# GpSimd's DMA queue in place of SyncE's for the preparations of chunks 4 to 9 of a recurrent attention kernel

## The chip, the cores and the metric

The kernel runs on one core of a Trainium2 chip. The metric is the device time of one execution in microseconds (us); less is better. Engines are named TensorE (PE in the profile), VectorE (DVE), ScalarE (ACT), GpSimd (POOL) and SyncE (SP). A DMA is begun by an instruction on the queue of one of these engines; SP does nothing but begin DMAs and wait.

## The reference

A linear recurrence over 768 steps for 4 x 8 heads of width 40, followed by two feed-forward parts over all 3072 tokens:

```python
for t in range(S):
    y[:, :, t] = einsum('bhd,bhde->bhe', rt, state)
    Sa = einsum('bhde,bhe->bhd', state, at)
    state = state * wt[:, :, None, :] - einsum('bhd,bhe->bhde', Sa, bt)
    state = state + einsum('bhd,bhe->bhde', vt, kt)
...
x = y.transpose(0, 2, 1, 3).reshape(B * S, H * D)
x = ((x @ w1) * (x @ w2) @ w3) @ w_out            # 320 -> 1024 -> 1024 -> 320
h = maximum(x @ w_in, 0)                          # 320 -> 2048
return h * h @ w_out2                             # 2048 -> 320
```

## The kernel before, in words

The recurrence is cut into 24 chunks of 32 steps. A chunk c needs a **preparation** that does not depend on the state. `prep` (L816) loads the chunk's image of k, b, a and w (`prep_load` L525: `im` at L538 in two parts, or for chunks 1, 2, 3 and 5 one load with w in it at L531; `iw`, the w part, at L548), scans w twice on VectorE (`prep_scan` L550: `suf` L553, `wi` L563, which at its end begins the load of the next chunk's `iw`), multiplies a by `wi` (L575) and k and b by `suf` (four of L581) on GpSimd (VectorE for chunks 0 to 3), and stores both to DRAM (`AW_d`, L582 and L583). `prep_pq` (L585) multiplies them on TensorE (L594); ScalarE copies one part to `Pn` (L598), VectorE transposes the other (`qt`, L599), GpSimd masks it from chunk 4 on (L601), and it is stored as `Q_d` (L602). `prep_kb` (L604) transposes k and b on TensorE (L611), ScalarE copies them to `kn` (L615), and they are stored as `KB_d` (L616). `im`, `iw`, `wi`, `qt` and `kn` have one buffer each from chunk 4 on (chunk 5 alone has another for `im`). `solve` (L621) inverts the triangular systems of four chunks at once, in a chain of small VectorE instructions (L653, L656).

The **state** then goes through each chunk in order: `do_x0` (L732, matmuls L739, copy X0 L741), `do_sa` (L744: L749, copy SA L751), `do_sat` (L753: L756, L758, L761), `do_l` (L763: L769, L774), `do_z` (L778), `do_ys` (L788: matmuls L797, results L805 and L809, store L812). Their inputs come back from DRAM by `load_x` (L703), `load_rv` (L722) and `load_y` (L712), all on SP's queue.

**Beside it** the weights come in and are decoded. `fetch` (L295) loads 64-bit words by SP (L319) into `raw` or `early` buffers; ScalarE (L325, L326) and VectorE (L328, L330) make float32 of them. w3 and w_out are folded into one matrix (L459), w1 and w2 are split in two parts (`split_w` L334, `split_r` L343, with subtractions on GpSimd), and from then on the first feed-forward part is worked in tiles of 256 tokens (`a_tile` L373: `ab` L370, `px` L428) as they leave the recurrence. These pieces stand in a list (`Fill` L73); `stage` (L827) writes one step of the recurrence and then pulls pieces worth so many ns from the list. The second feed-forward part (`ph` L370, `po` L994) follows at the end.

TensorE's order is that of the program, written by hand: `OPENING` (L28) holds the preparations 0 to 4, `BETWEEN` (L32) puts those of 5 to 9 between the steps of chunks 0 to 3, and from chunk 4 on the loop at L874 prepares chunk c + 6. All other engines' orders, SP's and POOL's too, come from a list scheduler with priorities, and an instruction that waits holds all behind it on its engine.

The queue on which a preparation begins its DMAs is a variable, `q_["prep"]` (L523). It is SP's from the start, and the loop sets it to POOL's at L880, where it prepares chunk 10, the first of its own. So all DMAs of L531, L538, L548, L582, L583, L602 and L616 are SP's for chunks 0 to 9 and POOL's after them, but for `iw` of chunk 10, which the scan of chunk 9 begins on SP.

Of the kernel before, what the change touches and what calls it, by code (L numbers as in the profile page):

```python
# [243 lines left out]
def body(tc, img, rv, rd, vn, vp, raw, w1, w2, w3t, wo, win, wo2, ident, maskt, out, dbg=None):  # L244
    nc = tc.nc
    mm = nc.tensor.matmul
    act, dve, pool, sp = nc.scalar, nc.vector, nc.gpsimd, nc.sync

    with (
# [12 lines left out]
        with right, tc.manual_schedule(engines={mybir.EngineType.PE}):  # L262
# [229 lines left out]
            with (  # L492
# [30 lines left out]
                q_ = {"prep": sp}  # L523
# [292 lines left out]
                def prep(p, eng=pool):  # L816
                    with tc.high_priority(offset=SECOND):
                        if p not in pr:
                            prep_load(p)
                        prep_scan(p)  # L820
                        prep_mul(p, eng)

                def solve_all(k, blocks=1):
                    with tc.high_priority(offset=SECOND):
                        return [it() for it in solve(k, blocks)][C // blocks + 3]

                def stage(fn, *a, gap=0):  # L827
                    with tc.high_priority(offset=FIRST):
                        fn(*a)
                    fill.pull(gap)  # L830
# [11 lines left out]

                def run(what):
                    for op, *a in what:
                        if op == "prep":
                            prep(a[0], dve if a[0] in PD else pool)
                        elif op == "pq":
                            stage(prep_pq, a[0], a[0] % 4)
                        elif op == "kb":
                            stage(prep_kb, *a)  # L850
                        elif op == "corner":
                            for b in range(2):
                                if len(a) == 1 or a[1] == b:
                                    stage(corner, a[0], b)
                        elif op == "solve":
                            marks[a[0]] = solve_all(a[0], 1 if a[0] else 2)
                        elif op == "pull":
                            fill.pull(a[0])
                run(OPENING)
                solved = marks[0]  # L860
                YI = at.tile([128, NU, 72], F32, name="YI")
# [12 lines left out]
                for c in range(NCH):  # L874
                    last = c == NCH - 1
                    p = c + 6
                    gaps = (GAP0, GAP1, GAP2, GAP3)[c] if c < 4 else GAPS if c < CUT[0] else GAPM if c < CUT[1] else GAPE
                    more = lambda name: run(BETWEEN.get((c, name), ()))
                    if c > 3 and p < NCH:
                        q_["prep"] = pool  # L880
                        prep(p)
                    more("start")
                    stage(do_x0, c, gap=gaps[0])
                    if not last:
                        stage(load_x, c + 1)
                    more("x0")
                    stage(do_sa, c, gap=gaps[1])
                    more("sa")
                    stage(do_sat, c, gap=gaps[2])
                    more("sat")  # L890
                    stage(do_l, c, gap=gaps[3])
                    if not last:
                        stage(load_rv, c + 1)
                    more("l")
                    if c:
                        stage(do_z, c, gap=gaps[4])
                        more("z")
                    if c > 3 and p < NCH:
                        stage(prep_pq, p, p % 4, gap=gaps[5])
                        stage(prep_kb, p, gap=gaps[6])  # L900
                        if p % 4 == 3:
                            solve_all(p // 4)
                    stage(do_ys, c, last, gap=gaps[7])
                    if not last:
                        stage(load_y, c + 1)
                    more("ys")
                    if c % 2:
                        a_tile(c // 2)
# [225 lines left out]
```

## Time and profile before

| | |
|---|---|
| median of 3 runs | 1076.19 us (1075.29 to 1082.97) |
| profiled execution | 1078.62 us, span 1076.7 us |
| TensorE busy | 917.4 us (85%) |
| VectorE busy | 714.0 us (66%) |
| ScalarE busy | 442.1 us (41%) |
| GpSimd busy | 233.3 us (22%) |

The span is the time from the first to the last instruction of the profiled execution; its own time is 1.9 us longer, and 2.4 us over the median of the runs. The chain that ended last is 52% TensorE, 23% VectorE and 12% DMA. Busy times leave out the issue of DMAs; a wait is named by what came last before it ended.

### The profile page before, as it was taken

Reading aid. Unit: us, or ns where it says so; the run is one execution under the profiler, and the core shown is the slowest. Engines: PE = TensorE matmul, PEld = TensorE weight load, DVE = VectorE, ACT = ScalarE, POOL = GpSimd, SP = SyncE. Lnnn points to the kernel's source line nnn. Section 1 sums busy time; section 2 is a strip of 40 time slices with the busy share of each in tenths; the row PEclk is TensorE's granted clock in tenths of the full one; section 3 lists DMA queues with packets and bytes.
Section 4 is the critical chain, followed back from the end, with each engine's and each line's share of the span. In section 5 each row is a group of like instructions: output and inputs, shape, how many; then the busy total and the mean of one; then the engine's idle time right before and its main releaser. Section 6 shows DMA issues by size and latency. Waiting matters only on the chain.

```text
span 1076.7 us, 29204 instructions
## 1 busy us (share of the span) xinstructions
PE 917.4 (85%) x12240; PEld 823.3 (76%) x12240; DVE 714.0 (66%) x1399; ACT 442.1 (41%) x942; POOL 233.3 (22%) x304
## 2 busy tenths in 40 slices
PE   1327866689989898988999989879999999999997
PEld 1315544588888888887899879868989889898886
DVE  6864879958975996798589344897455554444432
ACT  2424555343434323433343333785433333333332
POOL 0261224433343343434200000562000000000000
PEclk9999988899999899989999999999999999999999
DMA  8976775666666567765744542666122221000001
GB/s 211 312 228 181 215 238 152 163 177 161 168 158 166 147 154 170 173 152 146 182 119 110 129 97 63 159 182 126 30 61 49 63 48 25 2 25 1 18 8 27
DMA packets 208922, 134.44 MB, mean 125 GB/s; under 512 B 143742, under 2 KB 184063, under 8 KB 208369
## 3 DMA queue, kind: packets, MB, share of 16 engines
q1 hardware_dynamic: 201424, 110.61, 40.3%
q0 software_dynamic: 7072, 21.57, 7.2%
q8 instruction: 98, 1.61, 0.7%
q10 hardware_dynamic: 288, 0.33, 0.1%
q14 instruction: 40, 0.32, 0.1%
HBM read 99.27 MB, written 33.19 MB: 123 GB/s over the span
## 4 chain that ended last, share of the span: by engine, by line
PE 52%; DVE 23%; DMA 12%; issue 4%; ACT 4%; SPq 2%; POOL 2%; ACTq 0%; DVEq 0%; POOLq 0%
PE ph L370 15%; PE po L994 15%; PE ab L370 9%; PE px L428 4%; DVE tmp L653 4%; DVE T L656 4%; PE pat L797 2%; DVE wst L328 2%; DVE yst L809 2%; DVE RX L805 2%; DMA im<-img 2%; DMA raw<-w3t 2%; PE pat L769 2%; DMA AW_d<-wi 2%; PE pat L782 1%
## 5 line engine op out<-in xcount | busy, mean ns | idle before, releaser
L994 PE MATMUL po<-wuh,rl 128*128 128x320 f32 x384 | 117.2, 308 | 1.7 <-DVE rl L981 1.7
L994 PE MATMUL po<-wul,rh 128*128 128x320 f32 x384 | 118.3, 308 | 0.0
L994 PE MATMUL po<-wuh,rh 128*128 128x320 f32 x384 | 118.0, 308 | 0.0
L370 PE MATMUL ab<-xh,w1h 128*128 128x256 f32 x192 | 60.0, 313 | 24.6 <-DVE g L402 23.8
L407 ACT CAST gh<-g 128x256 fp32r<-128x256 f32 x96 | 38.9, 405 | 99.2 <-DVE g L402 99.1
L370 PE MATMUL ph<-xh,wih 128*128 128x512 f32 x192 | 76.0, 396 | 2.8 <-issue 2.8
L370 PE MATMUL ph<-xh,wil 128*128 128x512 f32 x192 | 75.7, 394 | 0.0
L370 PE MATMUL ph<-xl,wih 128*128 128x512 f32 x192 | 75.6, 394 | 0.0
L994 PEld LDWEIGHTS po<-wul,rh 128*128 128x128 f32 x384 | 72.0, 188 | 4.3
L994 PEld LDWEIGHTS po<-wuh,rh 128*128 128x128 f32 x384 | 72.0, 188 | 3.8
L994 PEld LDWEIGHTS po<-wuh,rl 128*128 128x128 f32 x384 | 71.7, 188 | 2.4 <-DVE rl L981 2.2
L428 PE MATMUL px<-wph,gh 128*128 128x320 f32 x192 | 65.6, 342 | 2.7 <-ACT gh L407 2.7
L656 DVE TENSOR_TENSOR T<-T,tmp 128x31 f32<-128x31 f32 (+20 forms) x170 | 65.6, 386 | 3.0
L797 PE MATMUL pat<-YI,YR 128*40 128x72 f32 (+1 forms) x1536 | 57.4, 237 | 11.5 <-ACT kn L615 6.7
L653 DVE TENSOR_TENSOR tmp<-PT,T 128x31 f32<-128x31 f32 (+20 forms) x170 | 64.9, 382 | 3.5
L408 DVE TENSOR_TENSOR gl<-g,gh 128x256 fp32r<-128x256 f32 x96 | 45.1, 470 | 33.1 <-ACT gh L407 32.9
L581 POOL TENSOR_TENSOR im<-im,suf 104x256 f32<-104x256 f32 x80 | 65.6, 849 | 0.0
L797 PEld LDWEIGHTS pat<-YI,YR 128*40 128x40 f32 x1536 | 53.1, 125 | 16.1 <-ACT kn L615 7.3
L428 PE MATMUL px<-wph,gl 128*128 128x320 f32 x192 | 61.3, 319 | 0.8 <-DVE gl L408 0.7
L428 PE MATMUL px<-wpl,gh 128*128 128x320 f32 x192 | 60.9, 317 | 0.0
L370 PE MATMUL ph<-xq,wir 128*128 128x512 f32 x192 | 60.3, 394 | 0.0
L401 ACT COPY a_sb<-ab 128x256 f32<-128x256 f32 x96 | 35.6, 371 | 58.6 <-PE ab L370 58.1
(539 smaller groups left out, 2452.6 us busy)
## 6 DMA issues: line engine op xcount, KB each, us to landing
raw<-w3t SPq DMA_DIRECT2D x16, 512.0 KB
YR<-KB_d SPq DMA_DIRECT2D x48, 160.0 KB
im<-img POOLq DMA_DIRECT2D x28, 240.0 KB, 4.6
wt<-AW_d SPq DMA_DIRECT2D x24, 214.5 KB
raw<-wo SPq DMA_DIRECT2D x16, 320.0 KB
RX<-vp SPq DMA_DIRECT2D x24, 208.0 KB
vs<-rv SPq DMA_DIRECT2D x24, 208.0 KB
KB_d<-kn POOLq DMA_DIRECT2D x14, 320.0 KB, 5.6
```

Of the source, the lines that this page charges most:

```text
L328: dve.scalar_tensor_tensor(out=ou, in0=ou, scalar=3, in1=lo, op0=ALU.logical_shift_left, op1=ALU.bitwise_or)
L370: mm(out=ps, lhsT=seq[i][0], rhs=seq[i][1], start=(i == 0), stop=(i == 7))
L401: act.copy(out=a_sb, in_=ps[:, 0])
L407: act.copy(out=t["gh"][:, ff], in_=g)
L408: dve.tensor_tensor(out=t["gl"][:, ff], in0=g, in1=t["gh"][:, ff], op=ALU.subtract)
L428: mm(out=ps, lhsT=a_, rhs=b_, start=(k == 0 and i == 0), stop=(k == 7 and i == 2))
L581: eng.tensor_tensor(out=kb[:, g, :, :, j], in0=kb[:, g, :, :, j], in1=sg, op=ALU.mult)
L653: dve.tensor_tensor(out=tv, in0=Pv[:, :, s, s + 1:n].unsqueeze(3).to_broadcast(sh), in1=Tv[:, :, s, 0:s + 1].unsqueeze(2).to_broadcast(sh) ...
L656: return dve.tensor_tensor(out=o, in0=o, in1=tv, op=ALU.subtract).ins
L769: mm(out=ps[q:q + 64, 0, 32 * i - q // 2:32 * i - q // 2 + 64], lhsT=vs[0:104, i], rhs=RT[0:104, :, i], start=True, stop=True, tile_positi ...
L797: mm(out=ps[64 * y:64 * y + D, b, 72 * z:72 * z + n], lhsT=YR[:, u], rhs=YI[:, u, 0:n], start=True, stop=True, tile_position=(0, 64 * y))
L994: mm(out=po[j][g], lhsT=a_, rhs=b_, start=(ff == 0 and i == 0), stop=(ff == 15 and i == 2))
```

## The change

The queue is chosen for each entry of the two lists by the chunk's number, and the line in the loop goes:

```diff
                 def run(what):
                     for op, *a in what:
+                        q_["prep"] = sp if a[0] < 4 else pool
                         if op == "prep":
                             prep(a[0], dve if a[0] in PD else pool)
                         elif op == "pq":
...
                     if c > 3 and p < NCH:
-                        q_["prep"] = pool
                         prep(p)
                     more("start")
```

The loads of chunks 0 to 3 are begun ahead of `run` (L832 to L837), on SP as before. The last entry of `BETWEEN` that runs, `("pull", 1000)` of chunk 3, leaves POOL's queue in the variable.

## Rows read from the trace of the kernel before

**Rows 1.** Busy time in four stretches: PE, PEld, DVE, ACT, POOL, then clock, DMA share.

```profile
60.00:140.00 80.00, 46.27 (x1241) 35.52 (x1231) 48.37 (x86) 31.18 (x69) 25.31 (x24) 0.94 0.74 205
140.00:220.00 80.00, 57.19 (x903) 44.67 (x903) 71.98 (x136) 42.95 (x91) 32.49 (x35) 0.82 0.68 184
220.00:300.00 80.00, 71.33 (x1318) 65.52 (x1316) 63.19 (x141) 29.49 (x70) 29.13 (x44) 1.00 0.65 162
300.00:600.00 300.00, 274.26 (x5089) 253.62 (x5089) 230.00 (x531) 115.86 (x273) 93.50 (x144) 0.95 0.61 153
```

**Rows 2.** Waits of TensorE, 0 to 230 us: total, times, longest.

```profile
PE pat L756 <- ACT SA L751: 18.0, 3, 8.7
...
PE pat L594 <- POOL im L575: 10.2, 1, 10.2
...
PE pat L797 <- ACT kn L615: 6.3, 1, 6.3
```

**Rows 3.** Waits of SP's queue, 0 to 200 us.

```profile
SPq L548 <- DVE wi L563: 8.6, 4, 3.7
...
SPq L602 <- POOL qt L601: 6.7, 3, 5.6
...
SPq L616 <- ACT kn L615: 6.0, 1, 6.0
```

**Rows 4.** SP's issues in order of time: start, duration, instruction.

```profile
68.40 0.35 SPq L602 DMA_DIRECT2D Q_d<-qt  x1
...
70.94 1.50 SPq L319 DMA_DIRECT2D raw<-w3t  x3
...
77.71 0.40 SPq L319 DMA_DIRECT2D raw<-w3t  x1
```

**Rows 5.** ScalarE in order of time; in brackets the idle time before.

```profile
82.60 0.67 ACT L326 ACTIVATE raw<-raw 128x512 uint32<-128x512 uint32 x1 [2.12 <-DMA raw<-w3t]
...
83.17 0.40 ACT L751 COPY SA<-pat 128x320 f32<-128x320 f32 x1
...
101.67 0.75 ACT L615 COPY kn<-pat 128x320 f32<-128x320 f32 x2 [4.47 <-DMA KB_d<-kn]
```

**Rows 6.** TensorE in order of time.

```profile
74.28 1.29 PE L749 MATMUL pat<-X,tt 32*32 32x40 f32 x64
...
83.63 1.10 PE L756 MATMUL pat<-idt,SA 128*104 128x128 f32 x4 [8.06 <-ACT SA L751]
```

**Rows 7.** DMA issues on POOL in the main loop, in order of time.

```profile
231.85 0.62 POOL L602 DMA_DIRECT2D Q_d<-qt  x1 [0.30 <-POOL qt L601]
232.46 1.02 POOL L538 DMA_DIRECT2D im<-img  x2
233.47 0.56 POOL L616 DMA_DIRECT2D KB_d<-kn  x1
```

**Rows 8.** VectorE in order of time.

```profile
64.31 2.37 DVE L330 SCALAR_TENSOR_TENSOR wst<-raw,wst 128x512 uint32<-128x512 uint32 x3
...
68.34 1.24 DVE L563 TENSOR_TENSOR_SCAN wi<-im,inv 104x528 f32<-104x528 f32 x1
```

**Rows 9.** GpSimd in order of time.

```profile
57.39 8.75 POOL L581 TENSOR_TENSOR im<-im,suf 104x256 f32<-104x256 f32 x4
66.10 2.27 POOL L601 TENSOR_TENSOR qt<-qt,msk 128x256 f32<-128x256 f32 x1
68.34 3.65 POOL L581 TENSOR_TENSOR im<-im,suf 104x256 f32<-104x256 f32 x4
71.94 1.17 POOL L575 TENSOR_TENSOR im<-im,wi 104x512 f32<-104x512 f32 x1
```

**Rows 10.** The chain that ended last: start, duration, what.

```profile
97.39 4.17 DMA KB_d<-kn
```

**Rows 11.** DMA issues on POOL by line: KB each, median us to landing.

```profile
im<-img POOLq DMA_DIRECT2D x28, 240.0 KB, 4.6
...
KB_d<-kn POOLq DMA_DIRECT2D x14, 320.0 KB, 5.6
```

## The prediction

> **What bounds the kernel now.** I read the busy time by stage first, because the change touches the first 200 us and little else. From 300 to 600 us TensorE is busy 274.26 of 300 us [rows 1], and its program order is fixed by hand, so the end moves only when the early stages move. From 60 to 140 us TensorE is busy 46.27 of 80 us, from 140 to 220 us 57.19 of 80, from 220 to 300 us 71.33 of 80 [rows 1]. What can be won is thus at most 33.7 + 22.8 us of idle TensorE between 60 and 220 us. In the second of these stages VectorE is busy 71.98 of 80 us: there it is the next limit, and there are only 8 us of slack in it.
>
> Second, who TensorE waited for, up to 230 us: 18.0 us for the copy of SA (8.7 the longest), 10.2 us for GpSimd's `im` in the preparation of chunk 5, 6.3 us for the copy of `kn` [rows 2]. Third, what held SP's queue, since the change takes work out of it. Between 0 and 200 us it stood 8.6 us for the scan `wi`, 6.7 us for GpSimd's `qt`, 6.0 us for the copy of `kn` [rows 3]: 21.3 us, all waits of stores and loads of preparations of chunks 4 to 9, and all of them in front of weight loads that were free to go.
>
> The clearest place is 62 to 84 us. SP stands 5.6 us, until 68.40, for the `Q_d` store of chunk 4, which needs GpSimd's `qt` [rows 3, 4]; the three loads of w3t go behind it at 70.94, and the fourth at 77.71, when VectorE has freed the first buffer [rows 4]. ScalarE decodes these loads in order; it waits 2.12 us for the fourth and only at 83.17 comes to the copy of SA behind it [rows 5]. TensorE had finished SA's matmuls at 74.28 + 1.29 = 75.6 us and waited 8.06 us for that copy [rows 6].
>
> **The change part by part.** From the code, the DMAs that go from SP to POOL are, for chunks 4, 6, 7, 8 and 9, two of `iw`, two of `im`, two of `AW_d`, one `Q_d` and one `KB_d`; for chunk 5 one load and four stores; and two `iw` of chunk 10, which are fetched in the scan of chunk 9. That is 40 + 5 + 2 = 47. Nothing is added or removed, and no byte moves that did not move before. `corner`, `solve` and `pull` also pass the new line, but begin no transfer of this queue; from chunk 4 of the main loop on the queue is POOL's as before.
>
> On SP an issue costs some 0.35 us (`Q_d` at 68.40 [rows 4]), so 47 x 0.35 = 16 us of SP's time go, and the 21.3 us of waits with them. On POOL an issue costs 0.51 to 0.62 us (1.02 for two of `im`, 0.56 for `KB_d`, 0.62 for `Q_d` [rows 7]), so POOL gets 47 x 0.55 = 26 us. It is busy 25.31 of 80 us and 32.49 of 80 in the two stages [rows 1]; most of the 26 us lie in idle time, and cost something where GpSimd itself is waited for.
>
> *The stall at 62.8.* Without the `Q_d` wait SP goes on at 62.8 with the loads of chunk 1's x0 (some 2.1 us, as between the end of `Q_d` at 68.75 and 70.94) and could issue w3t at 64.9. The buffers bind now: VectorE's last pass over three staged blocks runs 64.31 to 66.7 [rows 8], so the third load goes at 66.7 in place of 71.97. That is 5.3 us earlier. The fourth hangs on the first by the same decode, so ScalarE gets to SA 5.3 us earlier, at 77.9, still behind the matmuls' end at 75.6. I take -5.3 us. Bounds: -7.6 (the whole of 83.17 - 75.6) and 0 (if ScalarE's order puts another late load ahead).
>
> *Preparation of chunk 5.* TensorE waits for `im` of L575, 71.94 + 1.17 = 73.1 us. GpSimd works without a gap from 57.39: four L581 that take 8.75 us, `qt` 2.27, four more L581 (chunk 6) 3.65, then L575 [rows 9]. It could not run before VectorE's `wi` of 68.34 + 1.24 = 69.6 [rows 8]. The moved issues among these (`Q_d` and `KB_d` of chunk 4, two `im` of chunk 6) cost 4 x 0.55 = 2.2 us if all come before L575; if L575 is put ahead of chunk 6's L581, it gains 71.94 - 69.6 = 2.3. I take 0, bounds -2.3 and +2.2. What hides a loss here: nothing, as TensorE waits on it directly.
>
> *Stores of `KB_d`.* There is one `kn` buffer: ScalarE's next `kn` waits for the store of the last. At 97.39 the store landed after 4.17 us [rows 10], and ScalarE waited 4.47 us for it with X0's copy queued behind [rows 5]. On POOL this store comes behind `Q_d` and two `im` issues (231.85 to 233.47, 1.6 us later than `Q_d` [rows 7]), and its median landing is 5.6 us [rows 11], 1.4 more. At worst this is +3.0 us on TensorE's wait for X0, at best 0 when ScalarE's order changes. I take +2.
>
> *The rest of SP's waits* for `wi`, `qt` and `kn` is 21.3 - 5.6 = 15.7 us [rows 3, 4]: behind them lie loads whose buffers wait for VectorE anyhow, in the stage where it is 90% full [rows 1]. Bounds 0 and -15.7; the nearest row is VectorE's slack of 8 us, of which I take a quarter, -2.
>
> *From chunk 10 on* the queue is unchanged: 0.
>
> Sum: -5.3 + 0 + 2 - 2 = -5.3 us. The profiled execution took 1078.6 us (span 1076.7), 2.4 more than the median of the three runs, 1076.2. So 1073.3 against it, and 1070.9 as a median: 1071, 0.5% less.
>
> A rule that speaks against the change: during the run of 8.75 us GpSimd's four L581 took 2.4 times the 3.65 us of the next four [rows 9], beside VectorE's decode [rows 8]. The DMA issues of rows 7, in a stage where VectorE is 79% busy [rows 1], show no such stretch. The Trainium skill, "SBUF — State Buffer", section "SBUF: two separate sides", warns that GpSimd cannot write the descriptors of its DMAs while VectorE holds the port pair that they share, and gives some 3.1 us in place of 0.62 for one. If that held here, POOL would get an estimated 47 x 3.1 = 146 us and the sum would turn positive; the trace of the later chunks does not bear it out, and the third rival prices the same mechanism from rows.
>
> **The rivals.**
>
> *A larger gain.* All early stalls behind SP shrink, not the one. TensorE's longest waits beside the 8.06 us are 8.7 us for SA and 6.3 us for `kn` [rows 2], both where ScalarE's decode of weights was late. With half to all of these 15.0 us, say 11.7: 1078.6 - 5.3 - 11.7 = 1061.6, as a median 1059. For it: 21.3 us of waits leave SP [rows 3]. Against it: VectorE has 8 us of slack from 140 to 220 us [rows 1].
>
> *No change.* What is won before 140 us is waited for again at VectorE, whose work up to 220 us is the same; then 1076. For it: 71.98 of 80 us [rows 1]. Against: VectorE has 31.6 us idle from 60 to 140 us (48.37 busy of 80), into which work could move.
>
> *Slower: POOL's queue becomes the bound.* POOL takes its instructions in order, so a load waits for its buffer and the multiplication behind it for the landing. In the place from 66 to 73 us: `qt` ends at 68.37, `Q_d` 0.6, two `im` of chunk 6 1.0, landing 4.6 [rows 11], four L581 3.65, L575 ends at 68.4 + 0.6 + 1.0 + 4.6 + 3.65 + 1.17 = 79.4, against 73.1: +6.3 us at TensorE. The `KB_d` store adds up to 3.0 us in each of chunks 5 to 8, half of it 6.0; and issues stretched 2.4 times beside a full VectorE would put 47 x 0.55 x 1.4 = 36 us more on POOL, of which 5% on the path, 2. Together +14 us: 1092.6, as a median 1090. It decides as soon as L575 of chunk 5 ends more than 5.3 us later than now, after 78.4. For it: GpSimd is waited for already (10.2 us). Against: it is idle for more than half of both stages [rows 1], and only chunk 5 has TensorE waiting on it.
>
> That the change does not do what it says I exclude: with `a[0] < 4` every preparation of chunks 4 to 9 gets POOL's queue.
>
> **How the numbers follow.** Forecast 0.36, larger gain 0.28, no change 0.14, slower 0.22. A change of under 1% (10.8 us) can hardly be told from none here: 1065.4 and 1087.0 are the limits. Of the forecast's 0.36, 0.08 lie under 1065.4 (-7.6 - 2.3 + 0 - 2 = -11.9); of the slower case 0.03 stay under 1087. Faster 0.28 + 0.08 = 0.36; slower 0.19; within 1% 0.28 + 0.14 + 0.03 = 0.45. The range goes to 1054 (a little beyond the larger gain) and to 1090 (the slower case), with 0.1 outside at each end. The forecast's own range is 1064 to 1076.
>
> **What would show it.** Right: SP has no `Q_d` or `iw` in 60 to 170 us, w3t is issued near 66 us, ScalarE copies SA near 78 us and TensorE's wait for it is about 3 us in place of 8.06; `ys` of chunk 0 starts near 84 us. Wrong: L575 of chunk 5 ends after 76 us; POOL waits long for landings of `im` or for `kn`; VectorE is over 95% busy from 140 to 220 us and TensorE's 57 us there do not grow; or the gain before 140 us is gone at 300 us. The prediction falls if the time is under 1060 or over 1087.

## The result, and the profile after

| | before | after |
|---|---|---|
| median | 1075.74 us (1074.71 to 1082.97) | 1090.66 us (1086.0 to 1099.62) |
| ratio to before, 95% interval | | 1.0142 [1.0098, 1.0186] |
| profiled execution | 1078.62 us, span 1076.7 us | 1088.97 us, span 1087.1 us |
| GpSimd busy | 233.3 us | 254.2 us |
| bytes by POOL's DMA queue | 21.57 MB | 31.26 MB |
| `ys` of chunks 0, 1, 4 and 23 starts | 89.6, 120.4, 233.3, 671.6 | 88.5, 127.3, 241.0, 681.3 |
| last transpose of `solve(1)` starts | 214.35 | 224.24 |

The medians are of four runs each. The change costs 1.4%. The row of `ys` starts tells where. It wins 1.1 us at chunk 0, has lost 6.9 at chunk 1, 7.7 at chunk 4 and 9.7 at chunk 23; the span is 10.4 longer. So most of the loss arises between `ys` of chunk 0 and that of chunk 1, 38.9 us apart in place of 30.8, and is then carried along. Part of the 10.4 us is not a wait: the same 12240 matmuls in the same order kept TensorE busy for 921.4 us in place of 917.4, at a mean granted clock of 0.949 of full speed in place of 0.958.

Busy times of the kernel after, in the stretches of [rows 1]:

```profile
60.00:140.00 80.00, 43.39 (x1068) 34.10 (x1069) 51.05 (x79) 29.66 (x66) 36.98 (x47) 0.87 0.67 181
140.00:220.00 80.00, 55.05 (x893) 40.83 (x891) 72.30 (x136) 39.48 (x83) 36.35 (x44) 0.88 0.68 187
220.00:300.00 80.00, 71.38 (x1325) 66.21 (x1326) 60.20 (x136) 32.56 (x77) 29.30 (x44) 0.93 0.63 162
```

TensorE did 2.9 us less in the first stretch and 2.1 less in the second. GpSimd's busy time (fifth column) rose by 11.7 in the first; for this engine, unlike SP, it holds the DMA instructions too (the page counts 351 instructions in place of 304, the 47 that were moved). VectorE is as full in the second as it was. TensorE's waits, 0 to 230 us, against [rows 2]:

```profile
PE pat L749 <- ACT raw L326: 9.6, 1, 9.6
PE pat L749 <- ACT X L741: 8.7, 1, 8.7
PE pat L594 <- POOL im L575: 8.5, 1, 8.5
PE pat L756 <- ACT SA L751: 7.2, 2, 4.3
...
PE pat L797 <- DVE YI L774: 4.3, 1, 4.3
```

The wait for SA fell from 18.0 to 7.2 us, the way that was forecast. From 60 us on three others came up: X0 of chunk 1 (8.7), `YI` of chunk 0 (4.3), and 9.6 at chunk 4's `do_sa`. That last row names ScalarE, whose L326 had long been done; what ended then was `solve(1)`, below.

**Chunk 0: the gain, and where it went.** SP after, against [rows 4]:

```profile
66.74 8.05 SPq L319 DMA_DIRECT2D raw<-w3t  x4
```

The loads of w3t go from 66.74 on, 4.2 us earlier than before, as forecast. ScalarE after, in order of time:

```profile
74.75 0.67 ACT L326 ACTIVATE raw<-raw 128x512 uint32<-128x512 uint32 x1
75.58 0.42 ACT L751 COPY SA<-pat 128x320 f32<-128x320 f32 x1 [0.17 <-PE pat L749]
...
80.36 0.66 ACT L326 ACTIVATE raw<-raw 128x512 uint32<-128x512 uint32 x1 [2.47 <-DMA raw<-w3t]
```

SA is copied at 75.58 in place of 83.17 [rows 5]. But the decode of the fourth load of w3t, behind which SA stood before, now stands behind SA, at 80.36. It is only 82.60 - 80.36 = 2.2 us earlier. So the transfers' share of the 7.6 us is what lies between the fourth decodes or the third ones, 2 to 5 us, and ScalarE's order, which the scheduler wrote anew, gave the rest. TensorE after, against [rows 6]:

```profile
73.11 1.18 PE L594 MATMUL pat<-im 40*32 40x64 f32 x64 [8.50 <-POOL im L575]
...
78.20 1.07 PE L756 MATMUL pat<-idt,SA 128*104 128x128 f32 x4 [2.69 <-DVE qt L599]
...
88.48 3.73 PE L797 MATMUL pat<-YI,YR 128*40 128x72 f32 x60 [4.31 <-DVE YI L774]
```

L756 is 5.4 us earlier, `ys` of chunk 0 only 1.1: it waits 4.31 us for `YI`. The chain that ended last shows why:

```profile
68.52 0.72 POOL qt L601
...
69.73 7.28 DMA im<-img
...
80.72 0.70 POOL qt L601
...
81.70 0.60 POOL Q_d L602
...
82.81 2.25 DMA iw<-img
...
85.19 1.27 DVE suf L553
```

This is the queue of POOL at work. A load of `im` lands 7.28 us after its issue; L581 and `qt` follow; the store `Q_d` follows `qt`; and only behind them does POOL begin the load of `iw` of chunk 7, at 82.29, 2.0 us after the `wi` that it needs was done (80.24). VectorE, in its fixed order, waits for it with `YI` behind. Before, SP began that load as soon as `wi` was done, at 81.87. So the work in front of it had come forward by 5 us, and this load had not.

**Chunk 1: 6.9 us lost.** ScalarE after, then SP's weight loads after and before:

```profile
105.69 0.66 ACT L325 ACTIVATE wst<-early 128x512 f32<-128x512 f32 x1 [9.75 <-DMA early<-w]
...
106.80 0.42 ACT L741 ACTIVATE X<-pat 128x320 f32<-128x320 f32 x1
```

```profile
96.94 1.26 SPq L319 DMA_DIRECT2D early<-w  x2
```

```profile
98.27 0.37 SPq L319 DMA_DIRECT2D early<-w  x1
...
106.49 0.35 SPq L319 DMA_DIRECT2D early<-w  x1
```

The first block of w1 is begun 1.3 us earlier than before and decoded later, at 105.69 against 103.92. SP, with less else to do, now begins the second block with the first and not at 106.49, beside POOL's `im`; the DMA engines' share from 96 to 106 us is 1.01, before 0.94. And ScalarE's new order puts this decode ahead of X0, which it used to follow, and the decode of the second block ahead of SA. X0 comes at 106.80 in place of 102.31, SA at 110.11 in place of 105.05. When the same kernel was run again (e11), the first block was decoded at 103.18, no later than before, and X0 came at 104.28; but the second block then held SA to 111.62. What both executions share is the order. Then VectorE after, and GpSimd after:

```profile
109.75 0.68 DVE L330 SCALAR_TENSOR_TENSOR wst<-early,wst 128x512 uint32<-128x512 uint32 x1
110.35 5.76 DVE L330 SCALAR_TENSOR_TENSOR wst<-raw,wst 128x512 uint32<-128x512 uint32 x1
```

```profile
109.99 0.55 POOL L616 DMA_DIRECT2D KB_d<-kn  x1 [10.63 <-ACT kn L615]
110.56 1.19 POOL L575 TENSOR_TENSOR im<-im,wi 104x512 f32<-104x512 f32 x1
111.70 2.62 POOL L581 TENSOR_TENSOR im<-im,suf 104x256 f32<-104x256 f32 x4
114.28 1.28 POOL L341 TENSOR_TENSOR w1l<-wst,w1h 128x512 fp32r<-128x512 f32 x1
```

An instruction of 0.68 us takes 5.76, for as long as GpSimd works without a gap (110.56 to 115.56). It frees the buffer of the next load of w3t, which SP begins at 116.19. ScalarE waits for this load with the copy of `YR` behind it, and TensorE waits for `YR`; ScalarE and TensorE after:

```profile
122.27 0.66 ACT L326 ACTIVATE raw<-raw 128x512 uint32<-128x512 uint32 x1 [6.92 <-DMA raw<-w3t]
```

```profile
127.35 0.46 PE L797 MATMUL pat<-YI,YR 128*40 128x72 f32 x2 [3.44 <-ACT YR L785]
```

Before, `YR` was copied at 117.15, after at 126.61. Of the 6.9 us, 4.5 are there when TensorE goes on behind X0 (L749 at 107.27 in place of 102.81), and 2.5 come after it.

SP's queue shows where its waits went. Before and after, 0 to 200 us:

```profile
SPq L319 <- DVE wst L330: 17.9, 7, 4.1
```

```profile
SPq L319 <- DVE wst L330: 39.5, 12, 5.9
```

The waits of [rows 3] left it, 21.3 us; its waits for VectorE to free a buffer of a weight load grew by 21.6. The loads behind were not free to go.

**Chunk 4: paid at `solve(1)`.** VectorE before and after, first and last transposes of `solve(1)`:

```profile
128.88 2.10 DVE L646 STREAM_TRANSPOSE PT<-Pn 128x256 f32<-128x256 f32 x4
...
214.35 0.60 DVE L659 STREAM_TRANSPOSE tt<-T 128x256 f32<-128x256 f32 x1
```

```profile
136.86 2.17 DVE L646 STREAM_TRANSPOSE PT<-Pn 128x256 f32<-128x256 f32 x4
...
224.24 0.62 DVE L659 STREAM_TRANSPOSE tt<-T 128x256 f32<-128x256 f32 x1
```

`solve(1)` starts 8.0 us later and takes 1.9 longer (87.4 against 85.5). TensorE, which used to come to chunk 4's `do_sa` 1.6 us before its end, now waits 9.6, before and after:

```profile
215.10 1.29 PE L749 MATMUL pat<-X,tt 32*32 32x40 f32 x64 [1.58 <-DVE tt L659]
```

```profile
225.01 1.29 PE L749 MATMUL pat<-X,tt 32*32 32x40 f32 x64 [9.62 <-ACT raw L326]
```

Theory C, from here on: the end of `solve(1)` on a full VectorE sets chunk 4, and with it the span.

### The profile page after: what moved, and what is told of

It is laid out like the page before. It is cut to its first block, busy times and chain, and to the rows that moved or that the text cites. A ratio compares the mean times of both kernels' runs of the same rounds, so it can differ in the third digit from the quotient of the medians.

```text
span 1087.1 us, 29216 instructions
## 1 busy us (share of the span) xinstructions
PE 921.4 (85%) x12240; PEld 827.4 (76%) x12240; DVE 717.2 (66%) x1399; ACT 442.3 (41%) x942; POOL 254.2 (23%) x351
## 3 DMA queue, kind: packets, MB, share of 16 engines
q0 software_dynamic: 10144, 31.26, 10.1%
## 4 chain that ended last, share of the span: by engine, by line
PE 54%; DVE 22%; DMA 12%; issue 4%; ACT 3%; POOL 2%; SPq 1%; ACTq 0%; DVEq 0%; POOLq 0%
PE ph L370 17%; PE po L994 16%; PE ab L370 9%; DVE tmp L653 4%; PE px L428 4%; DVE T L656 4%; PE pat L797 3%; DMA im<-img 2%; DVE yst L809 2%; DVE RX L805 2%; PE pat L769 2%; DMA early<-wo 2%; DMA X_d<-yst 2%; DVE wst L328 2%; DMA early<-w 2%
## 5 line engine op out<-in xcount | busy, mean ns | idle before, releaser
L370 PE MATMUL ph<-xl,wih 128*128 128x512 f32 x192 | 76.7, 399 | 0.0
L653 DVE TENSOR_TENSOR tmp<-PT,T 128x31 f32<-128x31 f32 (+20 forms) x170 | 67.7, 398 | 3.4
L581 POOL TENSOR_TENSOR im<-im,suf 104x256 f32<-104x256 f32 x80 | 64.6, 837 | 5.9 <-DMA im<-img 3.0
L402 DVE TENSOR_TENSOR g<-a_sb,ab 128x256 f32<-128x256 f32 x96 | 39.9, 415 | 36.3 <-ACT a_sb L401 35.5
```

What stands on the lines that cost most here:

```text
L370: mm(out=ps, lhsT=seq[i][0], rhs=seq[i][1], start=(i == 0), stop=(i == 7))
L402: dve.tensor_tensor(out=g, in0=a_sb, in1=ps[:, 1], op=ALU.mult)
L581: eng.tensor_tensor(out=kb[:, g, :, :, j], in0=kb[:, g, :, :, j], in1=sg, op=ALU.mult)
L653: dve.tensor_tensor(out=tv, in0=Pv[:, :, s, s + 1:n].unsqueeze(3).to_broadcast(sh), in1=Tv[:, :, s, 0:s + 1].unsqueeze(2).to_broadcast(sh) ...
```

## The experiments

Each kernel was timed beside the kernel before on the same chip. In the expectations, A and A2 put the loss on the orders that the scheduler writes and on single waits in them, B on POOL's queue holding transfers back, C is the one above; D, E and F are told where they come up.

| kernel | ratio to before, 95% interval | span | last transpose of `solve(1)` | `ys` of chunks 1, 4 |
|---|---|---|---|---|
| before | | 1076.7 | 214.35 | 120.4, 233.3 |
| after | 1.0142 [1.0098, 1.0186] | 1087.1 | 224.24 | 127.3, 241.0 |
| after, again (e11) | 1.0109 [1.0066, 1.0151] | 1085.2 | 226.47 | 128.7, 243.7 |
| loads alone (e1) | 0.9957 [0.9927, 0.9987] | 1064.7 | 200.36 | 119.2, 227.3 |
| stores alone (e2) | 1.0005 [0.9968, 1.0043] | 1074.9 | 206.17 | 118.5, 233.3 |
| chunks 4, 5 (e3) | 1.0048 [1.002, 1.0075] | 1078.4 | 219.00 | 122.7, 239.8 |
| chunks 6 to 9 (e4) | 1.0035 [1.0008, 1.0062] | 1080.2 | 219.35 | 123.8, 238.9 |
| after, X0 first (e5) | 1.0107 [1.0049, 1.0165] | 1082.7 | 224.73 | 127.5, 243.6 |
| after, scan behind `YI` (e6) | 1.0103 [1.0069, 1.0136] | 1084.9 | 226.28 | 127.5, 244.1 |
| after, both (e7) | 1.0073 [1.0033, 1.0112] | 1081.9 | 219.10 | 122.5, 237.7 |
| loads alone, scan behind `YI` (e8) | 0.9974 [0.9944, 1.0004] | 1066.8 | 203.01 | 121.0, 230.8 |
| after, less decode on VectorE (e9) | 1.0075 [1.0046, 1.0103] | 1078.0 | 207.83 | 126.2, 234.4 |
| before, late end of `solve(1)` (e10) | 1.0076 [1.0051, 1.0101] | 1085.8 | 227.93 | 122.3, 245.8 |
| one store (e12) | 1.0012 [0.9985, 1.004] | 1074.4 | 216.65 | 122.2, 233.6 |
| after, one `KB_d` on SP (e13) | 1.007 [1.0036, 1.0104] | 1080.3 | 224.17 | 128.2, 242.9 |
| one store and two loads (e14) | 0.9991 [0.9964, 1.0018] | 1073.7 | 214.18 | 121.6, 234.1 |
| after, all `KB_d` on SP (e15) | 1.0042 [1.0009, 1.0074] | 1080.5 | 221.41 | 124.7, 239.6 |
| loads of `im` alone (e16) | 0.9955 [0.9922, 0.9987] | 1072.3 | 212.73 | 122.1, 232.2 |
| before, SA first (e17) | 1.0016 [0.999, 1.0043] | 1073.2 | 216.14 | 123.3, 234.3 |
| loads alone, SA first (e18) | 0.9931 [0.9907, 0.9954] | 1072.9 | 203.76 | 120.2, 234.3 |

The span and the starts are those of one execution. For e18 this one was the slowest of eleven, so its median, 1068.35 us, says more; for e1 it was the fastest of ten, for e10 the slowest of seven. Single executions scatter: in the five whose orders up to there are those of before, but for one swap on ScalarE in e17 (before, e10, e12, e14, e17), `ys` of chunk 1 starts between 120.4 and 123.3, and the last transpose, in e10 the first of twelve, between 214.2 and 218.8.

**Loads or stores, early or late chunks.** e1 gives the loads of `im` and `iw` alone to POOL, e2 the stores alone, e3 chunks 4 and 5, e4 chunks 6 to 9.

```diff
-                q_ = {"prep": sp}
+                q_ = {"prep": sp, "store": sp}
...
-                    q_["prep"].dma_start(out=Q_d[c], in_=qf.rearrange("p h t -> p (h t)"))
+                    q_["store"].dma_start(out=Q_d[c], in_=qf.rearrange("p h t -> p (h t)"))
```

> Only the loads (im, iw) of chunks 4 to 9 are begun by POOL, the stores by SP. Theory A (the loss is the order that the scheduler wrote on ScalarE: X0's copy of chunk 1 behind the decode of a late w1 load, in the changed kernel): in this kernel's ScalarE order X0 of chunk 1 stands ahead of that decode, so TensorE's wait for it is under 4 us in place of 8.7 and the time is 1072 to 1080. Theory B (POOL's in-order queue: loads wait there for buffers and behind landings): the loads are what waits, so most of the 14.9 us loss stays, 1086 or more.

> Only the stores (AW_d, Q_d, KB_d) of chunks 4 to 9 are begun by POOL, the loads by SP. Theory A: X0 of chunk 1 stands ahead of the w1 decode in ScalarE's order too, 1070 to 1080. Theory B: stores cost POOL 24 issues of 0.55 us, but no landing is waited for there; a third of the loss at most, 1076 to 1082. Parts that add up (e1 plus e2 losses equal the whole, 15 us) speak for B, parts that don't for A.

```diff
-                        q_["prep"] = sp if a[0] < 4 else pool
+                        q_["prep"] = pool if op != "pull" and a[0] in (4, 5) else sp
```

> Only chunks 4 and 5 go over POOL. Theory A: ScalarE's order at X0 of chunk 1 is that of the changed kernel (the decode of the first w1 block ahead of it), so the wait of 8 to 9 us at TensorE stays and the time is 1082 to 1095. Theory B: 13 of 47 transfers are moved, iw of chunk 7 is issued by SP again, so a third of the loss, 1077 to 1082.

> Only chunks 6 to 9 (and iw of chunk 10) go over POOL. Theory A: X0 of chunk 1 stands ahead of the decode, wait under 4 us, 1070 to 1080. Theory B: 32 of 47 transfers are moved and the waits of iw of chunk 7 behind im of chunk 6 are there, two thirds of the loss, 1084 to 1090.

The loads alone win 0.4%, the stores alone nothing that can be measured, the two together lose 1.1 to 1.4%. These parts don't add up, as costs of a queue would. Chunks 4 and 5 and chunks 6 to 9, which each move loads and stores together, each lose about a third; those two do add up within their intervals. In each of the four the list scheduler also wrote other orders for ScalarE and VectorE (in the kernel after, from 57 and from 27 us on; behind 230 us no instruction of theirs stands elsewhere). Of the orders that the expectations name, all four came: TensorE waits 3.5 to 3.9 us for X0 of chunk 1 in e1, e2 and e4, where it stands ahead of the first w1 decode, and 6.0 in e3, where it stands behind.

**Single waits.** e5 puts the decode of the first w1 block behind X0 of chunk 1 on ScalarE, e6 the scan `suf` of chunk 7 behind `YI` of chunk 0 on VectorE, e7 both; e8 makes the second edit in e1. In e6 and e8 the swap is all that differs in the orders; in e5 and e7 ScalarE's and VectorE's differ behind it too, up to 230 us.

```diff
+                with tc.issue_after(x0a[1]) if (tag, count["split"], 1 in x0a) == ("split", 1, True) else nullcontext():
                     act.activation(out=o, in_=hi.bitcast(F32), func=AF.Copy, scale=2.0 ** -112)
...
+                    with tc.issue_after(x0a["l", 0]) if c == 7 else nullcontext():
                         dve.tensor_tensor_scan(
```

> The changed kernel with one order on ScalarE: the decode of the first w1 block is written behind X0's copy of chunk 1. Theory A2 (the loss is the wait of 8.7 us for X0 of chunk 1, and the late ys of chunk 1 then lets solve of chunks 4 to 7 start and end 8 to 10 us later on a full VectorE): the wait is under 4 us, ys of chunk 1 begins before 123 us in place of 127.3, TensorE's wait for that solve at sa of chunk 4 is under 4 us in place of 9.6, and the time is 1076 to 1083. Theory B (POOL's queue itself): the wait moves elsewhere, 1087 or more.

> The changed kernel with one swap on VectorE: the scan of chunk 7, which waits for iw's landing from POOL's queue, stands behind the masked copy YI of chunk 0; all other engines' orders are the same. ys of chunk 0 begins 3 to 4 us earlier (near 85 us). Theory A2: X0 of chunk 1 then still waits for the w1 load, which SP begins behind loads that wait for that ys, so the 3 to 4 us are kept and the time is 1085 to 1088. Theory B: the same 3 to 4 us, since this one wait does come from POOL's queue. If the 3 us are lost at the next wait, 1090.

> Both orders of the two runs before. Theory A2: 1072 to 1080, level with the kernel before or under it. Theory B: 1084 or more.

> Loads alone over POOL (the kernel that took 1071.6) with the scan of chunk 7 behind YI of chunk 0. There TensorE waited 1.1 us for YI; 1069 to 1072 if that is all.

ScalarE in e5:

```profile
99.46 0.44 ACT L741 ACTIVATE X<-pat 128x320 f32<-128x320 f32 x1 [1.45 <-PE pat L739]
108.58 0.66 ACT L325 ACTIVATE wst<-early 128x512 f32<-128x512 f32 x1 [8.69 <-DMA early<-w]
```

X0 is free 7.3 us earlier, and the same load now holds SA behind it: TensorE waits 10.8 us there, and `ys` of chunk 1 stays at 127.5. In e6 `ys` of chunk 0 starts at 86.5, 2 us earlier, which is gone at chunk 1 too. Both together bring chunk 1 to 122.5 and the ratio to 1.0073, about half the loss, with an interval that still overlaps that of e11. Neither wait alone is the cause; ScalarE stands still on this load wherever it comes, and only the copies ahead of it escape. In e1 the second edit wins nothing.

Over all twenty kernels this order goes with the loss at chunk 1. Where SA of chunk 1 stands behind one w1 decode on ScalarE (eleven kernels), `ys` of chunk 1 starts 30.8 to 32.9 us after that of chunk 0; where it stands behind two (the other nine, e5 and e7 among them), 35.0 to 41.0. Two w1 blocks begun together are not enough for it: e1, e2, e4, e8, e16 and e18 begin them so and are of the eleven. But the nine are also those that move loads and stores of chunks 4 and 5, so that order and transfers are not told apart by this.

**Is it `solve(1)`?** e10 puts off nothing but its end: the orders of all engines are those of before up to there. e9 takes VectorE work out of the kernel after: it leaves out VectorE's part of the decode of five weight blocks.

```diff
-                        dve.transpose(out=tt.rearrange("p u t -> p t u")[:, 8 * j:8 * j + 8],
-                                      in_=square(T)[:, 8 * j:8 * j + 8])
+                        for _ in range(12 if (k, j) == (1, 3) else 1): dve.transpose(
+                            out=tt.rearrange("p u t -> p t u")[:, 8 * j:8 * j + 8], in_=square(T)[:, 8 * j:8 * j + 8])
```

> The kernel before, with the last transpose of solve(1) (L659) done twelve times in place of once; every engine's order up to there is that of before, so that nothing but the end of solve(1) is put off, by 4 to 7 us. Theory C: the whole of it is found again at the end, a span near 1082 (+5 us). Theory B, or any theory in which the middle of the kernel is held by transfers with room to spare: nothing of it is found again, a span within 2 us of 1076.7.

VectorE in e10, the first and the last of the twelve, and TensorE in e10:

```profile
218.78 0.61 DVE L659 STREAM_TRANSPOSE tt<-T 128x256 f32<-128x256 f32 x1
...
223.42 5.12 DVE L659 STREAM_TRANSPOSE tt<-T 128x256 f32<-128x256 f32 x8
```

```profile
228.68 1.29 PE L749 MATMUL pat<-X,tt 32*32 32x40 f32 x64 [10.73 <-DVE tt L659]
```

The end came 13.6 us later (228.54 against 214.95), more than the 4 to 7 meant. But the first of the twelve begins at 218.78 already, 4.4 us later than the one of before with the orders of before: that much is scatter of this execution, and TensorE comes as much later itself. The other eleven put the end off by 9.15 us, and TensorE's wait rose by these 9.15 us (10.73 against 1.58); the median rose by 0.76%, 8.2 us. What `solve(1)` alone ends late is paid, nearly whole. Behind the edit ScalarE's and VectorE's orders are other ones too; what these did is not separated.

```diff
-                    dve.scalar_tensor_tensor(out=ou, in0=ou, scalar=3, in1=lo, op0=ALU.logical_shift_left,
+                    if not (early and tag == "split" and count["split"] > 5): dve.scalar_tensor_tensor(out=ou, in0=ou, scalar=3, in1=lo, op0=ALU.logical_shift_left,
...
-                    dve.scalar_tensor_tensor(out=ou, in0=hi, scalar=0x80000000, in1=ou, op0=ALU.bitwise_and,
+                    if not (early and tag == "split" and count["split"] > 5): dve.scalar_tensor_tensor(out=ou, in0=hi, scalar=0x80000000, in1=ou, op0=ALU.bitwise_and,
```

> The kernel after, with the VectorE part of the decode (L328 and L330, ten instructions of 0.68 us) left out for the last five blocks of w1 and w2; what is computed with those blocks is then not the reference's. Theory C (the span is set by the end of solve(1) on a full VectorE, and lies 862 us behind its last transpose, as in the ten kernels so far): the last transpose of L659 comes about 7 us earlier than the 224.2 of after, near 217, and the span is about 5 to 7 us shorter, near 1081. Theory B (POOL's queue holds the transfers back throughout the middle): VectorE's work is not the limit, and the span stays within 3 us of 1087.

The last transpose came 16.4 us earlier, not 7; the orders changed too, from 170 us on. The span fell by 9.1, the ratio to 1.0075, with an interval that overlaps that of e11. TensorE waits no more for `solve(1)`, but still 8.6 us for an X0, 8.0 for `vs` and 7.2 for SA, all copies by ScalarE. So C holds up to the point where `solve(1)` is done in time; what would have to change beyond it was not tried. Over the twenty profiles of the table the span rises by 0.65 us for each us by which the last transpose starts later (correlation 0.89; with the ratios in place of the spans 0.60 us and 0.80). C is the main path and not the only one: in e13 `solve(1)` ends as late as after, and the span is 6.8 us shorter (4.9 against e11).

> The kernel after once more, beside the others on the same chip: a ratio between 1.010 and 1.018, with the last transpose of solve(1) near 224.

As expected; the loss is there again, with an interval that overlaps the first.

**Transfers alone, with the orders of before.** In e12 and e14 the orders of ScalarE, VectorE and TensorE are exactly those of before.

```diff
-                    q_["prep"].dma_start(out=Q_d[c], in_=qf.rearrange("p h t -> p (h t)"))
+                    (pool if c == 4 else q_["prep"]).dma_start(out=Q_d[c], in_=qf.rearrange("p h t -> p (h t)"))
```

> The kernel before, with one transfer alone moved to POOL: the store of Q_d of chunk 4, the one on which SP stood still at 62.8; the orders of ScalarE, VectorE and TensorE are those of before. The forecast's first term: w3t near 66, the copy of SA near 78, ys(0) near 85, and 3 to 5 us less at the end. Theory C: the same start, but the gain is kept only as far as solve(1) on VectorE ends earlier: a last transpose at 212 to 214 and 0 to 2 us less at the end.

SP in e12:

```profile
62.26 2.17 SPq L538 DMA_DIRECT2D im<-img  x1
...
65.42 3.36 SPq L705 DMA_DIRECT2D XL<-AW_d  x2
...
70.24 1.50 SPq L319 DMA_DIRECT2D raw<-w3t  x3
```

The store on which SP stood 5.6 us is gone, and w3t is begun 0.70 us earlier, not 5.3. Two DMA instructions of SP that took 0.32 us and 0.68 us (for two) before now take 2.17 and 3.36. e14 moves the two loads of `im` of chunk 6 as well:

```diff
-                        q_["prep"].dma_start(out=t[r], in_=img[c, r, 0:n])
+                        (pool if c in (6,) else q_["prep"]).dma_start(out=t[r], in_=img[c, r, 0:n])
```

> The kernel before with the store of Q_d of chunk 4 and the two loads of im of chunk 6 begun by POOL, nothing else; the orders of ScalarE, VectorE and TensorE are those of before. The forecast's first term alone, with the second thing on which SP stood still in the run with one store taken away too: w3t near 65, the copy of SA at 77 to 79, ys(0) at 84 to 86. If the 5 us are kept, the span is 1071 to 1073; theory C lets through only what solve(1) ends earlier, which with the order of before on VectorE is 0 to 3 us: a span of 1073 to 1077.

SP in e14:

```profile
57.89 7.24 SPq L727 DMA_DIRECT2D RT<-rv  x2
...
69.52 1.50 SPq L319 DMA_DIRECT2D raw<-w3t  x3
```

The wait went to the instruction before: two loads that took 0.66 us take 7.24, and w3t is begun at 69.52, SA copied at 82.57. In both, the time is that of before. This is the second cover of the first term: with the wait for `Q_d` gone, SP stands longer in other DMA instructions. What holds it there is not shown; that it is its own open transfers is a guess. Long ones occur in every kernel: before, a load of `YI` (L714) takes 2.8 us of SP in the median and up to 5.6. And e12 and e14 move one and three transfers where the change moves 47; no run moves all 47 with the orders of before.

**POOL's wait for `KB_d`.** e13 gives back the one store for which POOL stood 10.63 us, with ScalarE's order unchanged and VectorE's changed in part (117 to 165 us); e15 gives back all `KB_d` of chunks 4 to 9, with both orders changed from 107 us on.

```diff
-                    q_["prep"].dma_start(out=KB_d[c], in_=kn.rearrange("p g z y e -> p (g z y e)"))
+                    (sp if c in (6,) else q_["prep"]).dma_start(out=KB_d[c], in_=kn.rearrange("p g z y e -> p (g z y e)"))
```

> The kernel after with one transfer alone given back to SP: the store of KB_d of chunk 6, for which POOL stood still 10.6 us (to 109.99) with L575, L581 and L341 behind it. The orders of ScalarE and TensorE are those of after, VectorE's differs in 27 lines. Theory D (POOL's in-order wait makes ys(1) late): POOL runs L575 and L581 some 5 to 10 us earlier, no L330 beside them takes over 3 us, ys(1) comes at 123 to 125 in place of 127.5, and the last transpose of solve(1) and the span are 3 to 4 us earlier. Theory E (ScalarE's order: it waits for early<-w to 105.7 whatever POOL does): ys(1) stays at 127 and the span within 2 us of 1087.

> The kernel after with all stores of KB_d of chunks 4 to 9 given back to SP; loads and the stores of AW_d and Q_d stay with POOL. Theory D: POOL's waits for kn are the price of the change, so the time comes near that of the kernel with the loads alone on POOL: a ratio of 0.995 to 1.003. Theory E (each such set writes another order, and the order decides): a ratio anywhere from 1.003 to 1.014.

GpSimd in e13:

```profile
108.40 1.16 POOL L575 TENSOR_TENSOR im<-im,wi 104x512 f32<-104x512 f32 x1 [7.74 <-DMA im<-img]
```

The wait for `kn` gone, the landing of `im` holds the same instruction to 108.40 in place of 110.56. The stretched L330 is shorter (2.42 us at 113.33), but ScalarE waits 10.27 us for the w1 block as before, and `ys` of chunk 1 stays at 128.2. Theory D falls for this wait; E holds at chunk 1. Still the ratio is lower, 1.007, though its interval overlaps both of the kernel after; if that is a gain, it comes in some later part that no row here names. With all of `KB_d` back the ratio is 1.0042: the stores of `KB_d` on POOL, with the orders that come with them, are worth some 0.7% to 1.0%, the largest piece found, and the rest of the change is still no gain. This price hangs on the moved loads: in e2, where the loads stay with SP, all stores on POOL cost nothing that can be measured.

**What the faster set owes.** e16 gives POOL the loads of `im` alone, by the line of e14's second edit with chunks 4 to 9; that line is L538, so the one load of chunk 5 (L531) stays with SP.

> The kernel before with the loads of im of chunks 4 to 9 alone begun by POOL (iw and all stores stay with SP). If the gain of the kernel with both kinds of load on POOL comes from im, which holds 480 KB to 839 KB for each chunk and stays long in flight: a ratio of 0.993 to 0.998 and a last transpose of solve(1) at 200 to 206. If it comes from iw, or from the order written for that set: 0.998 to 1.005.

The same 0.4% as with `iw` too, though the last transpose started only 1.6 us earlier than before, at 212.73 and not at 200 to 206, which is within the scatter. So moving the loads of `im` is enough for that gain, and it does not come by way of `solve(1)` alone. Its orders differ from before as well; whether transfers or order give the 0.4% stays open.

**SA first.** e17 and e18 were to put the copy of SA of chunk 0 ahead of the fourth decode, in before and in e1.

```diff
+                with tc.issue_after(x0a["sa"]) if "sa" in x0a and "done" not in x0a and x0a.setdefault("done", 1) else nullcontext():
                     act.activation(out=o, in_=hi.bitcast(F32), func=AF.Copy, scale=2.0 ** -112)
```

> The kernel before with one thing changed: ScalarE's copy of SA of chunk 0 (L751) stands ahead of the fourth decode of w3t (L326) and not behind it, as it does in the kernel after; no transfer moves, and all other engines' orders are the same. Theory F (of the 7.6 us by which SA came earlier in the kernel after, the order gave what lies between the third and the fourth decode): SA near 80.1 in place of 83.2, ys(0) near 86.6 in place of 89.6. At the end: 3 us less if kept (a ratio near 0.997), nothing if solve(1) on VectorE still decides (0.999 to 1.001).

> The kernel with the loads alone on POOL, with the same swap on ScalarE: SA near 77.6 in place of 80.9, ys(0) near 84.5. If kept to the end, a ratio of 0.992 to 0.995; if solve(1) decides, that of the kernel without the swap, 0.994 to 0.998.

ScalarE in e17:

```profile
83.53 0.66 ACT L326 ACTIVATE raw<-raw 128x512 uint32<-128x512 uint32 x1 [3.80 <-DMA raw<-w3t]
84.09 0.41 ACT L751 COPY SA<-pat 128x320 f32<-128x320 f32 x1
84.40 0.68 ACT L326 ACTIVATE raw<-raw 128x512 uint32<-128x512 uint32 x1
```

The edit caught the wrong block. It acts on the first fetch written after SA, which is that of the third load: its decode stands behind SA at 84.40 and waits for nothing, while the last load, begun at 77.51, still holds SA, to 83.53. So F was not tested. What speaks for it are the rows of the kernels run: SA is copied between 75.5 and 76.7 us in all nine whose order has it ahead of the last load's decode, and between 80.8 and 84.1 in the other eleven; e1, which moves the loads and keeps the decode ahead of SA, copies SA at 80.87, 2.3 us earlier than before. The nine are again those that move loads and stores of chunks 4 and 5. e18 is the fastest kernel here, 0.7% under before, its interval overlapping that of e1.

## Why the prediction was wrong

It said 1071 us; the change gives 1090.66, just above its range and at the time of its slower rival.

*The stall at 62.8 (-5.3).* Right in size at TensorE (-5.4 at L756), but by luck: the cause was another, and so was what it is worth. e12 and e14 show that without the blamed store, and without the next thing in the way, w3t goes 0.7 and 1.4 us earlier: the longer DMA instructions on SP are a second cover under the first. Of the 7.6 us by which SA came earlier, the rows give 2 to 5 to the transfers and the rest to ScalarE's new order, which the forecast had kept. **The step that failed is here**: the 5.3 us at L756 were booked at the end without asking what `ys` of chunk 0 waits for next. That was `YI`, behind a load of `iw` that POOL began late, and 1.1 us were left (0.1 in e11).

*Preparation of chunk 5 (0).* Right in the number: L594 starts at 73.11 against 73.17. It is the sum of two shifts: L575 was put ahead of chunk 6's L581, as the lower bound has it, and VectorE's `wi` was done 2.2 us later (71.79 against 69.58).

*Stores of `KB_d` (+2).* Mis-sized. The forecast looked at the store's landing, which holds ScalarE; the wait that came was POOL's own for `kn`, with loads and multiplications behind it (10.63 us at 109.99). Between e15 and the kernel after lie 0.7 to 1.0%, 7 to 11 us, the changed orders included.

*The rest of SP's waits (-2).* No such gain came. "In front of weight loads that were free to go" was a wrong reading: 21.3 us of waits left SP's queue, and its waits for buffers that VectorE frees grew by 21.6. At chunk 1, where the sum had nothing but this term and the one before, the change lost 8.1 us between two `ys`. ScalarE's new order had two w1 decodes ahead of SA where one had been, and copies of the state waited with them.

*The slower rival* had the mechanism in part: POOL's order made `iw` of chunk 7 late and held L575 at 110. Its place was wrong, as L575 of chunk 5 did not move, and its stretched issues did not come (the rows of POOL above have 0.55 to 0.60 us for one); that its 14 us meet the measured time is luck. *No change* had the place: what counts is when VectorE is done with `solve(1)`.

What no part of the sum held: the scheduler wrote the orders of ScalarE and VectorE anew in every kernel that moved ten transfers or more. In the two that moved one and three (e12, e14) it did not, and nothing measurable happened; in the others the ratio lay between 0.993 and 1.014. How much of the 1.1 to 1.4% is order and how much is the queue stays open: the change was not run with the orders of before, nor the kernel before with those of after.

## What to carry to other kernels

Where a list scheduler orders the engines, a change of queue can change the orders of engines that it does not name: keep the orders fixed to learn what a transfer is worth, and don't book a stall's length at the end before the next two waits behind it have been read. A queue that stands on one instruction may stand in the next as soon as that wait is gone. On the queue of an engine that computes, a store that waits for another engine holds the loads and the work behind it: loads alone on GpSimd's queue won 0.4%, loads and stores together lost 1.1 to 1.4%.

## What was not expected of the hardware

An L330 of 0.68 us on VectorE took 5.76, 5.73 and 5.75 us in the kernel after, in e6 and in e11, each time beside an unbroken run of GpSimd of 5.0 us (L575, four L581, L341). In e13 no L330 beside the same run took more than 2.42 us, and in the kernel before three of them beside GpSimd's L581 took only 2.37 us together [rows 8, 9]; what makes the difference was not tried. The DMA instructions on SP, mostly 0.3 to 0.7 us long, took up to 7.24 us for two (e14); what holds them was not tried either.
